# Tile 0 centred from sums, key weights first, and a reordered tail of phase one in a transformer block's forward and backward kernel

## The chip, the core and the metric

The kernel runs on one core of one Trainium2 chip. The metric is the device time in microseconds (us) of one execution. The engines are TensorE (PE; its weight loads are PEld), VectorE (DVE), ScalarE (ACT), GpSimd (POOL) and SyncE (SP, which here only issues transfers).

## The reference

All inputs are bf16. The block has S = 2048 rows and D = 640 columns; H = 32 heads of 20; F = 1728.

```
layernorm(x) = (x - mean) / sqrt(var + 1e-5)            # per row
phi(t) = where(t > 0, t + 1, exp(t)) + 1e-6
q, k, v = split(layernorm(x) @ wqkv)                     # per head
kv = sum_s phi(k)^T v ;  z = sum_s phi(k)
h  = x + ((phi(q) @ kv) / (phi(q) . z + 1e-6)) @ wo
out = h + (silu(layernorm(h) @ w1) * (layernorm(h) @ w3)) @ w2
```

The kernel returns `out` and, for a given `grad_out`, the gradients of x, wqkv, wo, w1, w3 and w2: seven outputs.

## The kernel before, in words

Rows are worked on in 16 tiles of 128 (`ST`). The order of the work on each engine is the order in which the program is written: no scheduler reorders it, and the buffers and their waits are set by the builder.

**Start.** x tile 0 is loaded first, then `load_x` and `load_wq` calls load the other x tiles and halves of wqkv (320 columns each; halves 2 and 3 are the key weights). 34 matmuls on ones (`WARM`) run on PE meanwhile. Tile 0 gets its statistics on DVE (`ln1.part`: two `bn_stats`, one `bn_aggr`, then the variance plus epsilon, whose power -0.5 is taken by POOL, line 154). `center_first` subtracts the mean, 256 columns on DVE and 384 on ACT; the factor 1/sigma is applied later, as the scale of phi's exp and relu, and to x itself by `p1_scale` at t = 3. `RAW` is the number of tiles treated so. All others are normalised by `p1_norm` (subtract and multiply, in place).

**Phase one.** A loop over t multiplies tile t with the key weights (`p1_mm`), applies phi (exp and relu on ACT; the rest, lines 298 and 299, on DVE, held back in a list and done later by a step `R`) and stores `pk_all`. Tiles below 8 are transposed on PE (`p1_tr`) inside the product of the tile before; from 8 on by a transposing DMA on SP. `v_steps` writes out by hand which DVE work is done in which t: `S` statistics, `N` normalising, `C` scaling, `R` phi's rest; `A`, `B` and `L` normalise after phi, after `q_tile`, and last. `outs` and `trickle` give the bulk transfers for a t. `m_part` accumulates phi(k)^T x; the first chunks of the gradient product `ghh_chunk` (grad_out times w2 transposed) fill in.

**The end of phase one** is written out line by line: `q_tile` (phi(q) of a tile), `r_prod` and `r_row` (the denominators; on POOL and DVE), `m_part`, and `kvT_block` (five matmuls into a buffer of tag `big`, and a masked copy to `bd` on DVE, line 211). Then PSUM pool `p1p` (tags `tr` 2, `big` 2 double ones, `m` 2) is released, and pool `pap` (`mm` 4, `at` 2, `o2` 2) takes its place. Its first work is `q_late(10)`, with five transposes (`f2_mT`, line 717, tag `at`) between its halves.

**MLP.** Four chunks c of 512 rows times 14 chunks fc of 128 columns, n = 14 c + fc: `mlp` multiplies with w1 and w3, DVE multiplies the pairs (`mlp_pair`, line 829), and `mlp_ghh` makes the gradient chunk n + 2 (`AHEAD`) from n = 6 on. In between, `sides` puts the next chunk's attention output (`f2_at`, line 654), its normalising (`f2_hn`) and its transposed form (`f2_ht`), and `r_steps` the denominators of tiles 8 to 15 (`r_den`, lines 366 and 373, whose products from tile 8 on lie in PSUM buffers of tag `at`) and transfers.

The backward products follow and are not touched.

Of the kernel before, what the change touches and what calls it, by code (L numbers as in the profile page):

```python
# [55 lines left out]
def kernel(  # L56
# [128 lines left out]
    def load_x(a, b):  # L185
        dma(out=x_sb[:, a:b, :], in_=xS[:, a:b, :])

    load_x(1, 2)
    A.activation(sg[:], zero[:], AF.Exp)
    load_wq(2, 3)  # L190
    load_x(2, 3)
    load_wq(3, 4)
    load_x(3, 4)
# [45 lines left out]
    XT_DMA = 8  # L239
    WARM = 34  # L240
    RAW = 1

# [9 lines left out]
    def p1_tr(t, parts=((0, DT),)):  # L252
        xn = x_sb[:, t, :]
        for a, b in parts:
            tr = ps.tile([P, DT, P], BF16, name="tr", bufs=2)
            for c in range(a, b):
                T.transpose(tr[:, c, :], xn[:, c * P:(c + 1) * P], ident[:])

            A.copy(out=pqT[:, a:b, t * P:(t + 1) * P], in_=tr[:, a:b, :])  # L259
# [200 lines left out]
    load_g2T(0)  # L460
    load_x(8, 12)
    load_w2T(2 * P, 4 * P)
    load_wq(0, 2)
    load_x(12, ST)
    def warm_up(n, warm):
# [4 lines left out]
    def center(t, a=0, b=D):  # L470
        ln1.center(x_sb[:, t, a:b], x_sb[:, t, a:b], t)

    nmean = cp.tile([P, 1], F32, name="nmean")

    def center_first():
        V.tensor_scalar(out=nmean[:], in0=ln1.mv[:, 0, 0:1], scalar1=-1.0, scalar2=None, op0=ALU.mult)
        center(0, 0, 2 * P)
        A.activation(out=x_sb[:, 0, 2 * P:], in_=x_sb[:, 0, 2 * P:], func=AF.Identity, bias=nmean[:, 0:1])

# [4 lines left out]

    ln1.part(x_sb, 0, 0)
    ln1.part(x_sb, 0, 1, center_first)
    p1_tr(0, ((0, 2), (2, DT)))
    warm_up(8, p1_acc()[:, 0])
    stat(1)
    p1_norm(1)  # L490
    ln1.part(x_sb, 2, 0)
# [10 lines left out]
    def load_wo():  # L502
        dma(out=wo[:], in_=A_wo.rearrange("(c p) n -> p c n", p=P))

    trickle = {4: w13[0], 5: w13[1], 9: lambda: load_wq(4, 6), 12: w13[2], 14: w13[3]}

    R = None
    v_steps = {1: (R, ("N", 4)), 2: (("S", 5), R, ("N", 5)), 3: (("S", 6), R, ("N", 6), ("C", 0)),
               4: (("S", 7), R, ("N", 7), ("S", 8)), 5: (R, ("N", 8), ("S", 9)), 6: (R, ("N", 9), ("S", 10)),
               7: (("S", 11), R, R, ("A", 10), ("L", 11)), 8: (("S", 12), R, R, ("S", 13)),  # L510
               9: (("N", 13), R, ("S", 14), ("B", 12)), 10: (R, R, ("S", 15)), 11: (R, ("B", 14), ("L", 15))}
    V_OPS = {"S": stat, "N": p1_norm, "C": p1_scale}
# [8 lines left out]

    outs = {7: ((xn_out, 0, dma),), 8: ((group_out, 0),), 12: ((group_out, 1), (xn_out, 1, dma)), 13: ((group_out, 2),)}

# [3 lines left out]
    for t in range(ST):  # L527
        first = None
        if t < RAW:
            first = phi_tiles()  # L530
            kh = [ps.tile([P, 512], F32, name="k0", tag="m", bufs=2) for _ in range(2)]

            def act(i, j):
                A.activation(first[i][:, j * HD:(j + 1) * HD], kh[j][:, 0:HD], (AF.Exp, AF.Relu)[i],
                             scale=ln1.rs[:, t:t + 1])

            def between():
                act(0, 0)
                p1_tr(t + 1)
                act(1, 0)  # L540
            k = p1_mm(t, D, between, kh)
            act(0, 1)
            act(1, 1)
        else:
            k = p1_mm(t, D, (lambda: p1_tr(t + 1)) if t + 1 < XT_DMA else None)
# [80 lines left out]
    q_tile(8)  # L626
    kvT_block(1, big())
    r_row(4)
    r_prod(6)
    phi_rest()  # L630
    m_part(4, range(5, 11))
    q_tile(9)
    phi_rest()
# [111 lines left out]
    def f2_hn(t):  # L745
        hn[t] = (pf.tile([P, D], BF16, name="hn", tag="pql", bufs=4) if t == 2 else
                 pf.tile([P, D], BF16, name="hn", tag="h2", bufs=2) if t == 3 else
                 pf.tile([P, D], BF16, name="hn") if t % 2 else w2[:, FT, :])
        ln2.norm(hn[t][:], x_sb[:, t, :], t)
        if t < 2:  # L750
            f2_ht(t)
        for n in ((), (0, 1))[t] if t < 2 else (t,):
            dma(out=hn_v[:, n, :], in_=hn[n][:])
# [29 lines left out]
    def mlp(c, fc, between):  # L783

        k, i = divmod(fc, 2)
        n = c * FT + fc
        if n >= FILL - AHEAD:
            mlp_ghh(n + AHEAD)
        gp = mm5(w1, fc, hnT[c])
# [169 lines left out]
    def sides(c):  # L959
        side = ({}, {})  # L960
        for i in range(TPC):
            k0 = 3 * i - (i == TPC - 1) * (1 + (c == 1)) + (-2, 1, 0)[c]
            for k, pos, f in ((k0 + 2, 1, f2_at), (k0 + 3, 0, f2_hn), (k0 + 3, 1, f2_ht)):
                if c == 0 and f is f2_at:
                    if i == 0:
                        continue
                    f = f2_at0
                if k0 == -2 and f in (f2_at0, f2_hn, f2_ht):
                    k, pos = (k + 1, 0) if f is f2_at0 else (k + 1, pos)
# [11 lines left out]
    def r_end(t):  # L981
        r_scale(t)
        r_out(t)

    r_steps = [{0: ((load_x, 6, 8),), 1: ((r4_out, 0, 2),), 2: ((r_load, 8),), 3: ((load_w2T, 10 * P, F),), 4: ((r_load, 9), (r4_out, 2, 4)),
                5: ((r_store, 7, 8),),
# [6 lines left out]
    for c in range(SC):  # L993
# [4 lines left out]
        def run_side(pos, fc):  # L998
            if c + 1 < SC:
                for f, i in sorted(sides[c][pos].get(fc, ()), key=lambda x: (x[0] is f2_ht, x[1])):  # L1000
                    f((c + 1) * TPC + i)
# [597 lines left out]
```

## Time and profile before

| | |
|---|---|
| median of 3 runs | 822.12 us (821.39 to 822.13) |
| the profiled execution | 820.91 us |
| its span, first to last instruction | 819.1 us |
| PE busy | 814.1 us (99%) |
| DVE busy | 452.4 us (55%) |
| ACT busy | 323.6 us (40%) |
| POOL busy | 130.9 us (16%) |
| granted TensorE clock | 1.0 in the span's mean |

The profile is one execution taken by the hardware profiler. A line of its timeline gives the start in us, the duration, the engine and source line, the operation, what it writes and reads, and, in brackets, how long the engine stood idle before it and what ended that. Durations of consecutive instructions overlap, since an engine starts the next one before the last has written everything: starts, not durations, tell the pace. L12 is line 12 of the kernel before.

### The profile page before, as it was taken

The page shows a single profiled execution, that of the slowest core. Times are in us where ns is not written, and L with a number is a line of the kernel's source. Part 1 is how long each engine was busy: PE and PEld are TensorE (multiplying, and loading weights), DVE is VectorE, ACT ScalarE, POOL GpSimd, SP SyncE. Part 2 cuts the span into 40 slices and gives each one's busy share as a digit, 9 for nine tenths or more (in the row PEclk, how much of TensorE's full clock was granted, in tenths as well). Part 3 has the DMA queues.
Part 4 walks back from the last instruction along what each step waited for, and adds up shares of the span by engine and source line. Part 5 has one row for each costly group of instructions (what it writes and reads, how often), then busy time and mean ns, then how long its engine had stood idle before and what let it go on. Part 6 is the DMA issues. An engine that isn't in the chain of part 4 may idle for free.

```text
span 819.1 us, 13944 instructions
## 1 busy us (share of the span) xinstructions
PE 814.1 (99%) x5420; PEld 512.8 (63%) x5420; DVE 452.4 (55%) x973; ACT 323.6 (40%) x603; POOL 130.9 (16%) x193
## 2 busy tenths in 40 slices
PE   9999999999999999999999999999999999999998
PEld 6677544555555555777777777777777777544444
DVE  7859987998898566300057777772781544200000
ACT  7856688665565666011122212222212334211111
POOL 2233333333222212100001111110220000000000
PEclk9999999999999999999999999999999999999999
DMA  9899699796485556999977877259974997967751
GB/s 264 219 290 239 166 244 327 225 245 173 127 211 156 169 170 167 222 261 226 257 176 180 211 197 200 58 107 187 287 195 93 181 194 159 239 164 186 160 141 36
DMA packets 323873, 157.88 MB, mean 193 GB/s; under 512 B 242784, under 2 KB 317056, under 8 KB 323808
## 3 DMA queue, kind: packets, MB, share of 16 engines
q1 hardware_dynamic: 281040, 116.18, 61.6%
q0 software_dynamic: 7328, 24.48, 8.7%
q10 hardware_dynamic: 35440, 16.34, 7.7%
q8 instruction: 42, 0.69, 0.4%
q14 instruction: 23, 0.19, 0.1%
HBM read 47.09 MB, written 51.13 MB: 120 GB/s over the span
## 4 chain that ended last, share of the span: by engine, by line
PE 96%; DVE 2%; ACT 1%; issue 0%; DMA 0%; POOL 0%; ACTq 0%; DVEq 0%
PE mm L394 20%; PE job L1346 20%; PE ghn L1142 14%; PE gxn L1515 8%; PE gw L1097 7%; PE o L910 4%; PE o L856 3%; PE gwo L1230 3%; PE big L267 3%; PE gr L1199 3%; PE dkv L1452 3%; PE macc L429 2%; PE at L654 2%; PE mm L267 1%; PE dkv L1380 1%; DVE st L147 1%
## 5 line engine op out<-in xcount | busy, mean ns | idle before, releaser
L1346 PE MATMUL job<-gb,hnN 128*128 128x496 bf16 (+3 forms) x576 | 116.8, 366 | 0.0
L1142 PEld LDWEIGHTS <-ggb 128*128 128x128 bf16 x864 | 84.5, 98 | 32.8
L1346 PEld LDWEIGHTS <-hnN 128*128 128x128 bf16 x576 | 55.8, 98 | 61.0
L394 PE MATMUL mm<-pqT,w 128*128 128x512 bf16 x405 | 93.8, 379 | 0.1
L394 PEld LDWEIGHTS <-w 128*128 128x128 bf16 x540 | 52.5, 98 | 63.4 <-issue 1.4
L1350 ACT CAST obs<-job 128x496 bf16<-128x496 f32 (+4 forms) x56 | 28.5, 510 | 123.7 <-PE job L1346 120.9
L1142 PE MATMUL ghn<-w13a,ggb 128*128 128x320 bf16 x448 | 63.5, 299 | 0.0
L1157 DVE SCALAR_TENSOR_TENSOR wb<-gs,hnb 128x640 f32<-128x640 bf16 x16 | 13.2, 825 | 88.7 <-ACT gs L1154 88.7
L1142 PE MATMUL ghn<-w13b,ggb 128*128 128x320 bf16 x416 | 61.4, 299 | 0.0
L394 PE MATMUL mm<-g2T,w2T 128*128 128x512 bf16 x240 | 59.6, 379 | 0.0
L1097 PE MATMUL gw<-g,hb 128*128 128x320 bf16 x416 | 56.8, 299 | 0.0
L1207 POOL TENSOR_TENSOR sz<-Zb,g_h 128x640 f32<-128x640 bf16 x16 | 20.2, 1261 | 197.7 <-DVE g_h L1208 197.7
L1097 PEld LDWEIGHTS <-hb 128*128 128x128 bf16 x416 | 40.6, 98 | 16.0 <-issue 0.3
L419 ACT CAST ghh<-mm 128x512 bf16<-128x512 f32 x48 | 28.3, 589 | 47.7 <-PE mm L394 40.1
L793 ACT ACTIVATE sig<-mm 128x512 bf16<-128x512 f32 x56 | 33.9, 605 | 26.4 <-PE mm L394 21.1
L1154 ACT ACTIVATE gs<-ghn 128x640 bf16<-128x640 f32 x16 | 11.3, 704 | 78.8 <-PE ghn L1142 73.9
L394 PEld LDWEIGHTS <-w2T 128*128 128x128 bf16 x260 | 25.4, 98 | 23.4
L267 PEld LDWEIGHTS <-pqT 128*128 128x128 bf16 x320 | 30.7, 98 | 13.7 <-ACT pqT L259 1.5
L267 PE MATMUL big<-wqkv,pqT 128*128 128x320 bf16 x250 | 38.6, 299 | 0.6 <-ACT pqT L259 0.3
L1346 PEld LDWEIGHTS <-g 128*128 128x128 bf16 x320 | 31.0, 98 | 11.5
L829 DVE TENSOR_TENSOR gate<-gate,sig 128x1024 bf16<-128x1024 bf16 x28 | 19.3, 689 | 33.2 <-ACT gate L804 30.5
L910 PE MATMUL o<-w,hhT 128*128 128x320 bf16 x224 | 35.0, 299 | 0.0
(219 smaller groups left out, 1369.9 us busy)
## 6 DMA issues: line engine op xcount, KB each, us to landing
hh_d<-hhT SPq DMA_DIRECT2D x24, 256.0 KB, 2.7
gg_d<-gate POOLq DMA_DIRECT2D x24, 256.0 KB, 4.3
gg_d<-ghh POOLq DMA_DIRECT2D x24, 256.0 KB, 3.4
ggb<-gg_d SPq DMA_DIRECT2D x6, 896.0 KB, 5.4
ggb<-gg_d ACTq DMA_DIRECT2D x6, 832.0 KB, 5.7
ggb<-gg_d SPq DMA_DIRECT2D x2, 1728.0 KB, 12.7
x_sb<-in_A_x_dram SPq DMA_DIRECT2D x5, 640.0 KB, 5.9
pk_d<-pk_all SPq DMA_DIRECT2D x4, 640.0 KB, 6.6
```

What stands on the lines that cost most here:

```text
L267: T.matmul(acc, lhsT=pqT[:, c, t * P:(t + 1) * P], rhs=wqkv[:, c, n0:n0 + HD], start=(c == 0), stop=(c == DT - 1))
L394: T.matmul(acc[:], lhsT=w[:, c, fc * P:(fc + 1) * P], rhs=rhs[:, c, :], start=(c == 0), stop=(c == DT - 1))
L419: A.copy(out=ghh[n // 2][:, n % 2, :], in_=acc[:])
L793: A.activation(sig[:, i, :], gp[:], AF.Sigmoid)
L856: T.matmul(accs[i, j][:, 0:HD], lhsT=hhT[c][:, fc, i * P:(i + 1) * P], rhs=w2[:, fc, j * HD:(j + 1) * HD], start=(first and fc == 0), stop ...
L910: T.matmul(o2["ps"][:, 0:HD], lhsT=hhT[c][:, fc, i * P:(i + 1) * P], rhs=w2[:, fc, j * HD:(j + 1) * HD], start=(fc == 0), stop=(fc == FT - 1))
L1097: T.matmul(acc[:, j, 0:HD], lhsT=hb[b][:, t, i * P:(i + 1) * P], rhs=g2[:, t, j * HD:(j + 1) * HD], start=(t == 0), stop=(t == ST - 1))
L1142: T.matmul(acc[:, j, 0:HD], lhsT=ggb[t // 2][:, k, lo:lo + P], rhs=rhs[:, j * HD:(j + 1) * HD], start=(k == 0), stop=(k == NG - 1))
L1199: T.matmul(gr[t][:, j, 0:HD], lhsT=ghT[t][:, c, :], rhs=wT2[:, c, j * HD:(j + 1) * HD], start=(c == 0), stop=(c == DT - 1))
L1346: T.matmul(acc[:, 0:n], lhsT=lhs[:, t, m * P:(m + 1) * P], rhs=rhs(t), start=(t == 0), stop=(t == ST - 1))
L1350: A.copy(out=ob, in_=acc[:, 0:n])
L1515: T.matmul(acc[:, j, 0:HD], lhsT=g, rhs=wqT[:, k, j * HD:(j + 1) * HD], start=(k == 0), stop=(k == 14))
```

## The change

- Tile 0's mean is made of two half sums: ACT copies columns 320 to 639 with a running sum, DVE reduces columns 0 to 319; `nmean` is minus their sum over 640. The centred tile goes to a buffer `xc` and x tile 0 stays as it is; its statistics (`stat(0)`) follow.
- `RAW` is 2: tile 1 is only centred, and phi takes its scale. At t = 3, tile 0 is normalised in x and tile 1 is scaled.
- The two key weight halves are loaded ahead of x tiles 1 and 2. The warm-up matmuls are 30 and 4 instead of 34 and 8.
- The load of x tiles 8 to 15 is split after 10 instead of 12; a load of w3 moves from t = 5 to 7, a store of `pk_all` from t = 8 to 9; tile 14 is normalised before `q_tile(3)` instead of after.
- `kvT_block(1)` moves behind `r_row(4)`, `r_prod(6)`, `phi_rest` and six tiles of `m_part`.
- From tile 4 on `f2_ht` is called in `f2_hn`, not half a chunk later. From n = 14 on `mlp_ghh` works one chunk ahead, and n = 14 itself has none. A transposing load of w2 and the load `r_load(8)` change places.

```diff
@@ -185,11 +185,11 @@
     def load_x(a, b):
         dma(out=x_sb[:, a:b, :], in_=xS[:, a:b, :])
 
+    load_wq(2, 3)
     load_x(1, 2)
     A.activation(sg[:], zero[:], AF.Exp)
-    load_wq(2, 3)
+    load_wq(3, 4)
     load_x(2, 3)
-    load_wq(3, 4)
     load_x(3, 4)
     load_x(4, 8)
 
@@ -237,8 +237,8 @@
     Z = cp.tile([P, DT], F32, name="Z")
 
     XT_DMA = 8
-    WARM = 34
-    RAW = 1
+    WARM = 30
+    RAW = 2
 
     def on_act(t):
         return t > XT_DMA and t % 2 == 0
@@ -250,7 +250,7 @@
             dmaT(out=pqT[:, :, t * P:(t + 1) * P], in_=xn)
 
     def p1_tr(t, parts=((0, DT),)):
-        xn = x_sb[:, t, :]
+        xn = x_sb[:, t, :] if t else xc[:]
         for a, b in parts:
             tr = ps.tile([P, DT, P], BF16, name="tr", bufs=2)
             for c in range(a, b):
@@ -458,10 +458,10 @@
     zero_pads()
     load_w2T(0, 2 * P)
     load_g2T(0)
-    load_x(8, 12)
+    load_x(8, 10)
     load_w2T(2 * P, 4 * P)
     load_wq(0, 2)
-    load_x(12, ST)
+    load_x(10, ST)
     def warm_up(n, warm):
         for _ in range(n):
             T.matmul(warm[:, 0:P], lhsT=ones[:], rhs=ones[:], start=True, stop=True, skip_group_check=True)
@@ -470,24 +470,29 @@
     def center(t, a=0, b=D):
         ln1.center(x_sb[:, t, a:b], x_sb[:, t, a:b], t)
 
+    xc = p1.tile([P, D], BF16, name="rq", bufs=3)
+    sums = cp.tile([P, 2], F32, name="sums")
     nmean = cp.tile([P, 1], F32, name="nmean")
 
     def center_first():
-        V.tensor_scalar(out=nmean[:], in0=ln1.mv[:, 0, 0:1], scalar1=-1.0, scalar2=None, op0=ALU.mult)
-        center(0, 0, 2 * P)
-        A.activation(out=x_sb[:, 0, 2 * P:], in_=x_sb[:, 0, 2 * P:], func=AF.Identity, bias=nmean[:, 0:1])
+        x0 = x_sb[:, 0, :]
+        A.activation(out=xc[:, HD:], in_=x0[:, HD:], func=AF.Identity, accum_out=sums[:, 1:2])
+        V.reduce_sum(out=sums[:, 0:1], in_=x0[:, 0:HD], axis=AX.X)
+        V.tensor_scalar(out=nmean[:], in0=sums[:, 0:1], scalar1=sums[:, 1:2], scalar2=-1.0 / D, op0=ALU.add, op1=ALU.mult)
+        V.tensor_scalar(out=xc[:, 0:2 * P], in0=x0[:, 0:2 * P], scalar1=nmean[:, 0:1], scalar2=None, op0=ALU.add)
+        A.activation(out=xc[:, 2 * P:], in_=x0[:, 2 * P:], func=AF.Identity, bias=nmean[:, 0:1])
 
     def stat(t):
         ln1.run(x_sb, t, t + 1)
         if on_act(t):
             ln1.bias(t)
 
-    ln1.part(x_sb, 0, 0)
-    ln1.part(x_sb, 0, 1, center_first)
+    center_first()
+    stat(0)
     p1_tr(0, ((0, 2), (2, DT)))
-    warm_up(8, p1_acc()[:, 0])
-    stat(1)
-    p1_norm(1)
+    warm_up(4, p1_acc()[:, 0])
+    ln1.part(x_sb, 1, 0)
+    ln1.part(x_sb, 1, 1, lambda: center(1))
     ln1.part(x_sb, 2, 0)
     ln1.part(x_sb, 2, 1)
     ln1.part(x_sb, 3, 0)
@@ -502,13 +507,13 @@
     def load_wo():
         dma(out=wo[:], in_=A_wo.rearrange("(c p) n -> p c n", p=P))
 
-    trickle = {4: w13[0], 5: w13[1], 9: lambda: load_wq(4, 6), 12: w13[2], 14: w13[3]}
+    trickle = {4: w13[0], 7: w13[1], 9: lambda: load_wq(4, 6), 12: w13[2], 14: w13[3]}
 
     R = None
-    v_steps = {1: (R, ("N", 4)), 2: (("S", 5), R, ("N", 5)), 3: (("S", 6), R, ("N", 6), ("C", 0)),
+    v_steps = {1: (R, ("N", 4)), 2: (("S", 5), R, ("N", 5)), 3: (("S", 6), R, ("N", 6), ("N", 0), ("C", 1)),
                4: (("S", 7), R, ("N", 7), ("S", 8)), 5: (R, ("N", 8), ("S", 9)), 6: (R, ("N", 9), ("S", 10)),
                7: (("S", 11), R, R, ("A", 10), ("L", 11)), 8: (("S", 12), R, R, ("S", 13)),
-               9: (("N", 13), R, ("S", 14), ("B", 12)), 10: (R, R, ("S", 15)), 11: (R, ("B", 14), ("L", 15))}
+               9: (("N", 13), R, ("S", 14), ("B", 12)), 10: (R, R, ("S", 15)), 11: (R, ("A", 14), ("L", 15))}
     V_OPS = {"S": stat, "N": p1_norm, "C": p1_scale}
 
     def xn_out(g, q):
@@ -519,14 +524,14 @@
         sl = slice(g * TPC, (g + 1) * TPC)
         dma(out=pk_v[:, sl, :], in_=pk_all[:, sl, :])
 
-    outs = {7: ((xn_out, 0, dma),), 8: ((group_out, 0),), 12: ((group_out, 1), (xn_out, 1, dma)), 13: ((group_out, 2),)}
+    outs = {7: ((xn_out, 0, dma),), 9: ((group_out, 0),), 12: ((group_out, 1), (xn_out, 1, dma)), 13: ((group_out, 2),)}
 
     QT = (6, 7, 9, 11)
     M0 = {7: (0, 1, 2), 8: (3, 4, 5)}
     M0.update({t: (t - 3,) for t in range(9, ST)})
     for t in range(ST):
         first = None
-        if t < RAW:
+        if t == 0:
             first = phi_tiles()
             kh = [ps.tile([P, 512], F32, name="k0", tag="m", bufs=2) for _ in range(2)]
 
@@ -624,11 +629,11 @@
     r_prod(5)
     m_part(4, range(5))
     q_tile(8)
-    kvT_block(1, big())
     r_row(4)
     r_prod(6)
     phi_rest()
     m_part(4, range(5, 11))
+    kvT_block(1, big())
     q_tile(9)
     phi_rest()
     for j in range(2):
@@ -747,7 +752,7 @@
                  pf.tile([P, D], BF16, name="hn", tag="h2", bufs=2) if t == 3 else
                  pf.tile([P, D], BF16, name="hn") if t % 2 else w2[:, FT, :])
         ln2.norm(hn[t][:], x_sb[:, t, :], t)
-        if t < 2:
+        if t < 2 or t >= TPC:
             f2_ht(t)
         for n in ((), (0, 1))[t] if t < 2 else (t,):
             dma(out=hn_v[:, n, :], in_=hn[n][:])
@@ -784,8 +789,8 @@
 
         k, i = divmod(fc, 2)
         n = c * FT + fc
-        if n >= FILL - AHEAD:
-            mlp_ghh(n + AHEAD)
+        if FILL - AHEAD <= n < FT or n > FT:
+            mlp_ghh(n + (AHEAD if n < FT else 1))
         gp = mm5(w1, fc, hnT[c])
         if i == 0:
             pair[k] = [ew(name) for name in NAMES]
@@ -960,12 +965,12 @@
         side = ({}, {})
         for i in range(TPC):
             k0 = 3 * i - (i == TPC - 1) * (1 + (c == 1)) + (-2, 1, 0)[c]
-            for k, pos, f in ((k0 + 2, 1, f2_at), (k0 + 3, 0, f2_hn), (k0 + 3, 1, f2_ht)):
+            for k, pos, f in ((k0 + 2, 1, f2_at), (k0 + 3, 0, f2_hn)):
                 if c == 0 and f is f2_at:
                     if i == 0:
                         continue
                     f = f2_at0
-                if k0 == -2 and f in (f2_at0, f2_hn, f2_ht):
+                if k0 == -2 and f in (f2_at0, f2_hn):
                     k, pos = (k + 1, 0) if f is f2_at0 else (k + 1, pos)
                 if k >= 0:
                     side[pos].setdefault(k, []).append((f, i))
@@ -982,7 +987,7 @@
         r_scale(t)
         r_out(t)
 
-    r_steps = [{0: ((load_x, 6, 8),), 1: ((r4_out, 0, 2),), 2: ((r_load, 8),), 3: ((load_w2T, 10 * P, F),), 4: ((r_load, 9), (r4_out, 2, 4)),
+    r_steps = [{0: ((load_x, 6, 8),), 1: ((r4_out, 0, 2),), 2: ((load_w2T, 10 * P, F),), 3: ((r_load, 8),), 4: ((r_load, 9), (r4_out, 2, 4)),
                 5: ((r_store, 7, 8),),
                 10: ((xn_out, 2, dmaG),), 12: ((r_load, 10),)},
                {0: ((r_den, 8), (load_x, 8, 12)), 1: ((r_end, 8), (r_load, 11), (xn_out, 3, dmaG)), 2: ((r_den, 9),), 3: ((r_end, 9), (r_load, 12)),
@@ -997,7 +1002,7 @@
 
         def run_side(pos, fc):
             if c + 1 < SC:
-                for f, i in sorted(sides[c][pos].get(fc, ()), key=lambda x: (x[0] is f2_ht, x[1])):
+                for f, i in sorted(sides[c][pos].get(fc, ()), key=lambda x: x[1]):
                     f((c + 1) * TPC + i)
 
         for fc in range(FT):
```

## The prediction

> **What bounds the kernel now.** I read the page's busy shares first, then who TensorE (PE) waited for, then the timeline at the places the change touches.
>
> ```profile
> span 819.1 us, 13944 instructions
> PE 814.1 (99%) x5420; PEld 512.8 (63%) x5420; DVE 452.4 (55%) x973; ACT 323.6 (40%) x603; POOL 130.9 (16%) x193
> ...
> DVE  7859987998898566300057777772781544200000
> ```
>
> ```profile
> PE warm L467 <- DVE zero L124: 1.1, 1, 1.1
> PE big L267 <- ACT pqT L259: 0.3, 1, 0.3
> ```
>
> PE is never idle long, so its program order sets the end. A busy PE hides short waits, so I also took the start-to-start distances of consecutive matmuls against the pace of the long streams here (fifteen of 512 columns in 3.24 us, 0.216 each; ninety of 320 in 12.22, 0.136). By that, PE loses 4.1 us in the first 20 us and afterwards only in five places more than 0.1 us: 0.28 at 37.7, 0.25 at 96.0, 0.16 at 97.5, 0.28 at 102.0, 0.15 at 548.7. So the change can win at most the start plus about 1.1 us, and it loses whatever new pause it puts into PE's order. VectorE (DVE) is the engine to watch: its digits are 9 and 8 in many slices.
>
> The start:
>
> ```profile
> 3.19 0.89 DVE L147 BATCH_NORM_STATS2 st<-x_sb 128x6 f32<-128x320 bf16 x2 [1.93 <-DMA x_sb<-in_A_x_dram]
> ...
> 4.36 0.15 DVE L476 TENSOR_SCALAR nmean<-ln_mv 128x1 f32<-128x1 f32 x1
> 4.43 0.28 DVE L157 TENSOR_SCALAR x_sb<-x_sb,ln_mv 128x256 bf16<-128x256 bf16 x1
> 4.55 0.62 ACT L478 ACTIVATE x_sb<-x_sb,nmean 128x384 bf16<-128x384 bf16 x1 [2.25 <-DVE nmean L476]
> ...
> 4.76 0.96 PE L257 MATMUL tr<-ident,x_sb 128*128 128x128 bf16 x5
> ...
> 6.37 1.20 PE L267 MATMUL k<-wqkv,pqT 128*128 128x320 bf16 x5
> ```
>
> The reader sees the chain arrival, statistics, mean, centring, transposes, first product. The end of the first phase, in time order across engines:
>
> ```profile
> 68.61 0.47 PE L448 MATMUL bigx<-mT,wqkv 128*128 128x140 bf16 x5
> ...
> 72.56 0.29 DVE L211 TENSOR_TENSOR bd<-bigx,mask 128x140 bf16<-128x140 f32 x1
> ...
> 72.77 0.86 DVE L373 TENSOR_REDUCE rden<-pr 128x16 f32<-128x320 f32 x2
> ...
> 73.94 0.51 PE L717 MATMUL trm<-ident,hx 128*128 128x128 bf16 x5
> ...
> 75.46 0.31 DVE L298 TENSOR_SCALAR mq<-mq 128x640 bf16<-128x640 bf16 x1
> ...
> 76.29 0.32 DVE L298 TENSOR_SCALAR mq<-mq 128x640 bf16<-128x640 bf16 x1
> ```
>
> DVE runs almost four us behind PE here: the product of `kvT_block(1)` is done at 69.08, its masked copy (L211) starts at 72.56. And in the MLP's second chunk row:
>
> ```profile
> 143.00:184.80 41.80, 41.80 (x230) 22.31 (x229) 40.69 (x84) 26.41 (x50) 12.80 (x19) 1.00 0.87 236
> ```
>
> The columns are PE, PEld, DVE, ACT and POOL busy: DVE 40.69 of 41.80 us, as full as PE.
>
> **The change part by part.**
>
> *Tile 0's mean by sums.* Removed from the front of the chain: two statistics and an aggregate (3.19 to 4.33). In their place DVE reduces 320 elements (nearest row L373, 128x320: 0.48) beside ACT, which copies 320 with a running sum. ACT from SBUF took 0.62 for 384 and 0.92 for 640, so 0.54 for 320; the accumulator read behind L1154 takes 0.19 and starts 0.10 before its ACTIVATE ends. Sum: 3.19 + 0.54 + 0.09 = 3.83 against DVE's 3.67. `nmean` (0.15 + two hand-overs of 0.035) ends the wait: centring starts at 4.06 on DVE instead of 4.43, and on ACT 0.49 earlier. Transposes begin near 4.38 and the first product near 5.8 instead of 6.37. The shorter warm-ups (30 and 4) fill those two waits and cost nothing: 30 matmuls end by 4.3.
>
> *What becomes of that 0.5 us.* Tile 0's statistics now follow on DVE, and tile 1 is only centred, which takes it off POOL's power (L154, 0.55, for which DVE stood idle 0.67). DVE: centre 4.06, statistics 4.25 to 5.17, aggregate and variance to 5.47, statistics of tile 1, centring at 6.63, statistics of tile 2 at 6.99, against 7.02 before. So DVE is where it was, if x arrives. It may not: the weight half of 410 KB now goes ahead of tile 1, which landed at 3.58 before and the half at 5.81; in the new order tile 1 takes the half's place (5.4 to 5.8) and tile 2 the second half's place (6.9 to 7.35). DVE then shifts by 0 to +0.36; I take +0.15, between the two orders' landings. From 10.9 to 34.3 DVE has no pause but its own hand-overs, so this shift stays.
>
> *Tile 0 normalised late, tile 1 scaled late.* The step at t = 3 was one scaling (L263); it becomes a normalising (0.44, next start 0.36 later) and the scaling: +0.36 on the same full DVE. The cover is PE's reserve on DVE's transposes (0.54 at 21.5), which holds; it ends at the pause at 37.7, where PE waits for ACT's relu, which waited for DVE (ACT idle 0.97 before 36.73). There the DVE shift comes through whole: 0.36 + 0.15 = **+0.5 us**, ends 0.3 and 0.8. Tile 1's two ACT passes with a scale (0.79 against 0.70) add 0.18 to ACT early, which PE sees as 0.08 at most and within the same 0.5.
>
> *Transfers.* w3's first half (832 KB) goes from t = 5 to t = 7, the stores of `pk_all` from t = 8 to 9. That puts 832 KB instead of 640 KB in front of the transposed rows of tiles 12 and 13 on SP's queue; tile 12's landed 0.11 us before PE needed it at 40.1. 192 KB more at some 340 GB/s (the first loads ran at 326 to 349) is 0.55 us less 0.11 of reserve; the 0.5 from above delays rows and PE alike. Ends 0 and +0.45; I take **+0.15**. Tile 14's norm on ACT ahead of `q_tile(3)`: 0.92 us of ACT where PE's next need is over 1.2 us off: nothing. The x split, `load_w2T` before `r_load(8)`, and `f2_ht` beside `f2_hn`: these rows land earlier or chunks ahead of use: nothing, and at worst what stood behind them on SP moves by one issue (1.2 us) under a reserve of chunks.
>
> *`kvT_block(1)` behind `phi_rest` and six tiles of `m_part`.* PE's order loses nothing. But on DVE its masked copy moves behind `r_row(4)` (72.77 to 75.46) and the two operations of tile 8's phi (75.46 to 76.29). It starts 3.52 later, at 76.08, and ends at 76.37. Who waits: the copy frees a `big` pair, and the next PSUM pool's tiles come to lie on those of the old (2 `tr`, 2 double `big`, 2 `m` against 4 `mm`, 2 `at`, 2 `o2`). The trace's semaphores have the first transpose of `f2_mT` (L717, tag `at`) wait for DVE, and the only DVE reader of the old buffers is L211. Its reserve is 73.94 - 72.85 = 1.09. So 3.52 - 1.09 = **+2.4 us** of PE pause. If the pair were the other one, `q_late(10)`'s second half at 74.29 would wait instead: 2.1. Nothing later gives it back: DVE and ACT are again waiting for PE by 82 (DVE 0.58 before 81.85).
>
> By the rows, is PE as fast after such a pause? The 34 warm-up matmuls of 128 columns took 0.107 us each and the five of 320 at 6.37 took 1.20, at 7.69 0.84: the full pace came about 7.1 us, some 6 us after PE's first work. No pause after that exceeds 0.5 us, so no row shows a loss of pace. [...]
>
> *One gradient chunk less ahead.* From n = 14 the ghh chunk is made one ahead, not two: chunk 14 loses five 512-column matmuls (1.08 us) and PE arrives 1.08 earlier at all that follows, until the last chunks even it out. DVE is full until 184.8 and can follow by only 0.39 (its pause there). The tightest place is `f2_at` at 190.50, which takes a buffer that DVE's `r_red` (189.85, first half done 190.33) frees: reserve 0.16. So 1.08 - 0.39 - 0.16 = **+0.55 us**, ends 0 and 0.9. No other reserve under 1.08 lies between 143 and 330 us.
>
> **Sum.** 0.5 + 0.15 + 2.4 + 0.55 = +3.6 us. The profiled execution took 820.91 (span 819.1 + 1.8), so it would take 824.5. The three runs' median is 822.12, 1.2 above it; on that scale 825.7. With all low ends +2.4 (824.5), with all high ends +4.6 (826.7).
>
> **Rivals.**
> A, *not slower*: the masked copy gates nothing, because the pool hands `kvT_block(1)` a buffer that is covered late, or the wait is short. Place: L717 at 73.94; price: -2.4, leaving +1.2, 823.3, within 0.2%. It decides from a pause under 0.45 us. For it: the buffers are picked by the program's builder, which the trace doesn't show for the new order. Against: all eight places are reused within 2 us.
> B, *faster*: the 0.5 us of the earlier first product survives and no shift of DVE reaches PE, and A holds: -0.5, 821.6. Against it: DVE full from 10.9 to 34.3. Even with all later pauses gone it would be 820.5.
> C: after the 2.4 us pause PE works at the warm-up's pace for as long as at the start: up to half of 6 us, +3.0: 828.7. For it: the slow start; against: short pauses left the pace alone.
>
> **Numbers.** About 0.2% (1.64 us) is what a measurement of this kernel can tell from no change. Forecast 0.79, A 0.10, B 0.03, C 0.05, the rest slower for small reasons. Likeliest 825.7, its own range 824.4 to 826.8. To leave out no more than two in ten and take in A: 823.2 to 827.3. Slower 0.87, same 0.11, faster 0.02.
>
> **What would show it.** Right: PE idle over 2 us before L717, released by DVE's L211; that L211 starting right behind tile 8's L299; a pause of half a microsecond before `at` in the MLP's second chunk row; a first product near 5.8, and `q_tile(3)` yet later than 38.1. Wrong: no PE wait at L717, or its transposes starting at 73.9 or earlier.

## The result and the profile after

The changed kernel takes 828.32 us in the median of six runs (826.48 to 829.96); the kernel before, beside it, 821.77 (821.31 to 823.79). The ratio is 1.0076, with a 95% interval of 1.0060 to 1.0093: slower by 6.55 us, where the forecast was +3.6 and the range ended at 827.3. Five of the six runs have a mean granted clock of 0.997 or 0.998; the sixth, at 1.000, took 826.48. The profiled execution took 828.32 us (clock 0.998) with a span of 826.5, against 819.1 before.

The page after, its head and DVE's row of the 40 slices (20.7 us each):

```profile
span 826.5 us, 13891 instructions
...
PE 813.4 (98%) x5384; PEld 512.3 (62%) x5412; DVE 454.1 (55%) x975; ACT 324.8 (39%) x605; POOL 130.8 (16%) x193
...
DVE  7858898999888656400047777772681545200000
```

PE's busy time is that of before (814.1, within a few missing records). The span is 7.4 us longer, so nearly all of that is pauses or slow matmuls. Whom PE waited for after the change (engine, line, what it waited for: us in total, times, longest):

```profile
PE trm L722 <- DVE bd L211: 2.3, 1, 2.3
PE big L267 <- DMA pqT<-x_sb: 1.3, 1, 1.3
PE tr L257 <- DVE ln_ve L153: 1.2, 1, 1.2
PE warm L467 <- DVE zero L124: 1.1, 1, 1.1
PE trh L770 <- DVE hn L160: 0.6, 1, 0.6
PE tr L257 <- DVE x_sb L160: 0.5, 1, 0.5
PE mm L394 <- DMA pqT<-hn: 0.5, 1, 0.5
```

Before, only the line of the first warm-up exceeded 0.3 us. The new lines are the accounts of this document. (Lines behind 480 have moved by 5: L722 is the old L717, L770 the old L765.) Measured as in the prediction, by start-to-start distances of matmuls against the pace of long streams, the 7.4 us fall apart thus (rounded, they add up to 7.5):

| place in the changed kernel | us | forecast |
|---|---|---|
| start, as far as it reaches 40 us (`tr` waits; the first product is 1.1 us earlier and does not help) | 0.6 | 0.5 |
| rows of tile 14 at 45.1 us | 1.5 | 0.15 |
| `trm` at 75.9 us, waiting for L211 | 2.5 | 2.4 |
| matmuls at half pace, 79.0 to 82.5 us | 1.6 | 0 (rival C, +3.0) |
| `trh` and the matmul behind it, 101.8 to 105.2 us | 1.0 | 0 |
| MLP's second chunk row, at 196.4 us | 0.3 | 0.55 |

Each size is a difference between two single profiles. The experiments below show how much of them is the change's.

The forecast pause, in the timeline after:

```profile
75.33 0.84 PE L267 MATMUL mm<-wqkv,pqT 128*128 128x320 bf16 x5
...
76.43 0.97 DVE L380 TENSOR_TENSOR pql<-pql,rden 128x640 bf16<-128x640 bf16 x1
...
77.32 0.31 DVE L298 TENSOR_SCALAR mq<-mq 128x640 bf16<-128x640 bf16 x1
...
77.73 0.49 DVE L299 TENSOR_TENSOR hx<-mq,rq 128x640 bf16<-128x640 bf16 x1
78.14 0.30 DVE L211 TENSOR_TENSOR bd<-bigx,mask 128x140 bf16<-128x140 f32 x1
...
78.49 0.44 PE L722 MATMUL trm<-ident,hx 128*128 128x128 bf16 x5 [2.32 <-DVE bd L211]
```

The masked copy stands right behind tile 8's L299, as forecast, and PE's first transpose follows it by 0.05 us. What was not forecast comes next. Three stretches of the same trace (us of each, then PE, PEld, DVE, ACT and POOL busy with the number of instructions, then the granted clock, DMA share and GB/s):

```profile
75.63:79.04 3.41, 1.09 (x12) 0.74 (x10) 3.13 (x8) 0.56 (x3) 1.08 (x2) 1.00 1.09 213
79.04:82.46 3.42, 3.42 (x21) 2.50 (x19) 0.55 (x2) 2.72 (x7) 0.00 (x0) 0.50 0.76 275
82.46:85.87 3.41, 3.41 (x38) 2.73 (x36) 2.82 (x8) 2.15 (x7) 0.00 (x0) 1.00 0.02 5
```

PE was busy for 1.09 of the first 3.41 us; for the next 3.41 us the clock is 0.50, and the same matmul of 320 columns that starts every 0.136 us elsewhere starts every 0.267. By the clock alone that is half of 3.41, 1.7 us; against the same matmuls before, 1.6.

### The profile page after: what moved, and what is told of

It is laid out like the page before. It is cut to its first block, busy times and chain, and to the rows that moved or that the text cites. A ratio compares the mean times of both kernels' runs of the same rounds, so it can differ in the third digit from the quotient of the medians.

```text
span 826.5 us, 13891 instructions
## 1 busy us (share of the span) xinstructions
PE 813.4 (98%) x5384; PEld 512.3 (62%) x5412; DVE 454.1 (55%) x975; ACT 324.8 (39%) x605; POOL 130.8 (16%) x193
## 4 chain that ended last, share of the span: by engine, by line
PE 86%; DVE 10%; DMA 2%; issue 1%; ACT 1%; SPq 0%; POOL 0%; DVEq 0%; ACTq 0%
PE job L1351 19%; PE mm L394 16%; PE ghn L1147 14%; PE gxn L1520 8%; PE gw L1102 7%; PE o L861 3%; PE gwo L1235 3%; PE gr L1204 3%; PE dkv L1457 3%; PE o L915 2%; PE at L659 2%; DVE st L147 1%; DVE s L834 1%; PE macc L429 1%; PE mm L267 1%
## 5 line engine op out<-in xcount | busy, mean ns | idle before, releaser
L834 DVE TENSOR_TENSOR gate<-gate,sig 128x1024 bf16<-128x1024 bf16 x28 | 19.3, 689 | 34.6 <-ACT gate L809 31.9
```

Source lines behind the costliest of these rows:

```text
L834: V.tensor_tensor(out=out, in0=a, in1=b, op=alu)
```

## Experiments

All kernels of a group ran on one chip together with the kernel before; times are medians in us. Kernels named `b_` are the kernel before with one edit, those named `a_` are the changed kernel with one or several. The ratios are the record's own; they can differ from the quotient of the two medians, by up to 0.0007 (`a_t6_fill8`, `b_pool`).

| group | kernel | us | before beside it | ratio, 95% interval |
|---|---|---|---|---|
| 1 | `b_kvt` | 826.18 | 823.24 | 1.0031 (1.0018 to 1.0044) |
| 1 | `b_kvt_mid` | 824.75 | 823.24 | 1.0014 (1.0002 to 1.0026) |
| 1 | `a_kvt_back` | 825.13 | 823.24 | 1.0020 (1.0010 to 1.0031) |
| 1 | `a_warm` | 827.52 | 823.24 | 1.0050 (1.0033 to 1.0067) |
| 2 | `after_again` | 828.17 | 822.47 | 1.0070 (1.0057 to 1.0082) |
| 2 | `a_bulk_back` | 825.54 | 822.47 | 1.0041 (1.0027 to 1.0054) |
| 2 | `b_head` | 822.78 | 822.47 | 1.0007 (0.9998 to 1.0016) |
| 2 | `b_mlp` | 822.85 | 822.47 | 1.0002 (0.9993 to 1.0011) |
| 3 | `a_undo2` | 823.77 | 823.27 | 1.0011 (1.0003 to 1.0020) |
| 3 | `a_late` | 823.61 | 823.27 | 1.0007 (0.9998 to 1.0015) |
| 3 | `b_late` | 825.46 | 823.27 | 1.0030 (1.0017 to 1.0044) |
| 3 | `b_pool` | 824.70 | 823.27 | 1.0024 (1.0013 to 1.0035) |
| 4 | `b_t6` | 822.11 | 822.75 | 0.9992 (0.9982 to 1.0003) |
| 4 | `b_bulk` | 823.35 | 822.75 | 1.0012 (1.0001 to 1.0023) |
| 4 | `b_kvt_warm` | 824.77 | 822.75 | 1.0025 (1.0012 to 1.0038) |
| 4 | `a_t6` | 823.36 | 822.75 | 1.0006 (0.9997 to 1.0015) |
| 5 | `a_t6_fill8` | 823.09 | 822.56 | 1.0000 (0.9991 to 1.0010) |
| 5 | `b_few8` | 823.07 | 822.56 | 1.0005 (0.9995 to 1.0014) |

**The pause and the clock.** `b_kvt` moves the one call; `b_kvt_mid` moves it less far:

```diff
     q_tile(8)
-    kvT_block(1, big())
     r_row(4)
+    kvT_block(1, big())   # b_kvt_mid: here
     r_prod(6)
     phi_rest()
     m_part(4, range(5, 11))
+    kvT_block(1, big())   # b_kvt: here instead, as in the change
     q_tile(9)
```

> The kernel before with only kvT_block(1) moved behind r_row(4), r_prod(6), phi_rest and six tiles of m_part. Theory 1 (pause and clock): the masked copy L211 comes some 3.5 us later on DVE, PE pauses 2.4 us before the transposes of f2_mT, the granted clock falls to half for one stretch of 3.41 us behind the pause and takes another 1.7 us: +4.1 us, about 825.9 against 821.8, clock of the span about 0.998. Theory 2 (the pause alone; the slow matmuls of the changed kernel came from something else in it): +2.4 us, about 824.2, clock 1.000.

> The kernel before with kvT_block(1) moved less far, behind r_row(4) only. The masked copy starts 2.7 us later than before instead of 3.5; less the reserve of 1.09 us PE should pause about 1.6 us. If the clock falls only where most of a 3.41 us stretch is idle (1.6 is 47% of it): +1.6 us, about 823.4, clock 1.000. If any pause of more than a microsecond lets it fall: +3.3 us, about 825.1, clock 0.998.

In `b_kvt` PE loses 2.48 us before `trm`, as in the changed kernel. Its twelve runs fall into two halves: six at a clock of 0.998, median 827.07, and six at 1.000, median 825.16, 1.9 us apart, where half pace over 3.41 us gives 1.7. So both theories of the expectation were right in half of the runs each; theory 1 is the one that says why. In `b_kvt_mid` the pause is 1.65 us (forecast there: 1.6); of twelve runs one shows 0.998 and two 0.999. (0.999 need not mean a slow stretch in the work: in the profiled runs of `a_kvt_back` and `a_t6`, both at 0.999, the clock fell only for the last 0.9 us of the span, behind PE's last product.)

What decides in a given run? Wherever the clock's records show it change, it does so in steps of one grid of 3.41 us, whose place differs from run to run: in the changed kernel's profile at 3.95, 79.04, 82.46 and 826.56 us (22, 1 and 218 steps apart), in that of the kernel before at 7.09 and 819.46 (238 steps). Here is `b_kvt`, whose profiled run slowed down, by stretches of its grid:

```profile
74.91:78.32 3.41, 1.09 (x12) 0.77 (x11) 2.99 (x7) 0.56 (x2) 0.67 (x1) 1.00 1.12 230
78.32:81.73 3.41, 3.41 (x23) 2.72 (x21) 0.65 (x3) 2.30 (x7) 0.00 (x0) 0.50 0.86 246
```

And the changed kernel's second profile (`after_again`), in which the same pause of 2.48 us left the clock alone:

```profile
74.30:77.71 3.41, 2.70 (x20) 1.82 (x19) 3.27 (x7) 1.95 (x4) 2.08 (x3) 1.00 1.06 190
77.71:81.13 3.42, 1.80 (x18) 1.42 (x18) 2.18 (x6) 1.33 (x4) 0.00 (x0) 1.00 0.88 203
```

There the grid cut the pause in two, and PE was busy for 1.80 us of the emptier stretch (53%). The four profiled stretches that were followed by half pace in the midst of the work had PE busy for 1.09 and 1.09 (the changed kernel and `b_kvt`), 1.35 (`a_bulk_back`, at 5.3 us, where the start's two waits fell into one stretch) and 1.46 us (`b_pool`): 32 to 43%. The emptiest stretch that kept the clock is one of `a_kvt_back`, with 1.72 us (50%). `b_pool`'s and `a_kvt_back`'s:

```profile
30.53:33.94 3.41, 1.46 (x12) 0.83 (x10) 3.11 (x10) 1.07 (x2) 0.96 (x2) 1.00 1.10 151
33.94:37.35 3.41, 3.41 (x15) 1.85 (x14) 2.54 (x8) 1.34 (x3) 0.55 (x1) 0.50 1.03 351
...
45.50:48.91 3.41, 1.72 (x13) 1.19 (x13) 1.44 (x7) 0.66 (x3) 1.23 (x5) 1.00 1.12 285
48.91:52.33 3.42, 3.42 (x27) 2.45 (x26) 1.49 (x5) 2.54 (x4) 0.39 (x2) 1.00 1.06 412
```

The ends of the profiles, where PE runs out of work, agree. In the eighteen whose records show the clock fall there, it falls behind a stretch with 0 to 40% of work, and not behind the four stretches with 52 to 57% that stand one step earlier. So in these traces the bound lies between 43 and 50% of a stretch; the one with `b_kvt_mid`'s pause of 1.65 us had 56% in the profiled run and stays on the safe side of it. A stretch in which PE was idle for 57% (`b_pool`) was enough here; in the prediction's sum the pause of 2.4 us has no such cost.

`a_warm` and `b_kvt_warm` keep the pause but fill it with work that nobody reads:

```diff
             p1_half(acc[:, 0:HD], t, j * HD)
             if j == 0 and between is not None:
+                if t == 10:
+                    for _ in range(36):
+                        T.matmul(acc[:, HD:HD + P], lhsT=ident[:], rhs=ident[:], start=True, stop=True, skip_group_check=True)
                 between()
```

> The changed kernel with 36 matmuls of 128 columns, whose results nobody reads, put on PE right before the transposes of f2_mT, in unused columns of the PSUM tile of q_late(10)'s first half: 1.96 us of work at full pace inside the 2.4 us pause. The pause's end, set by DVE, stays. Theory 1: the clock stays at 1.000 and 1.7 us come back, about 826.6. Theory 2: no change, 828.3.

> The kernel before with only kvT_block(1) moved, and 36 matmuls whose results nobody reads in the pause. Theory 1: the pause's end stays where DVE sets it, +1.9 us as in the runs of b_kvt with the full clock, and the clock is 1.000 in all runs instead of six of twelve: ratio about 1.002 against 1.003. Rival (the clock has another cause): as many runs below 1.000 as b_kvt.

In `a_warm`, 36 matmuls take the place of the pause, and `trm` still waits for L211:

```profile
75.64 2.17 PE L696 MATMUL mm<-ident 128*128 128x128 bf16 x36
78.11 0.44 PE L725 MATMUL trm<-ident,hx 128*128 128x128 bf16 x5 [0.30 <-DVE bd L211]
```

All thirteen runs of the two kernels have a clock of 1.000, where `b_kvt` has six low clocks in twelve and the changed kernel eight in eleven. They lie within 1.0 us (`a_warm`) and 2.9 us (`b_kvt_warm`) of each other. `b_kvt_warm` has a median of 824.77, 2.0 us above before, and no second group. So the slow clock hangs on PE's idleness, and the later copy alone costs 2.0 us: theory 1 is shown. As a repair the filling wins little, since the wait for the copy stays: 1.0025 against `b_kvt`'s 1.0031. (`a_warm`'s 1.0050 against the changed kernel's 1.0076 and 1.0070 is not the clock's doing alone: the pause at 102 us, treated below, is gone there too.)

**Which part costs what.** The parts one at a time, and the change without its two costliest:

> The changed kernel once more, beside the kernels of this group. In the four kernels run so far the transfers of the first phase cost more pauses (30.6 us, 45 us, 104 to 107 us) than in the two profiles from before, so the change's cost is wanted from this group: ratio 1.006 to 1.009 if the larger part is the pause at f2_mT with the slow clock behind it (the clock below 1.000 in about half of the runs, as with kvT_block(1) alone, 1.8 us apart).

> The changed kernel with kvT_block(1) back in its old place. Theory 1: both the pause and the slow stretch go, -4.1 us, about 824.2 against 828.3, clock 1.000; the 1 us lost between 96 and 107 us stays if it has another cause and goes too (823.2) if it follows from the pause. Theory 2: -2.4 us, about 825.9.

> The changed kernel with the w3 half back at t = 5 and the first pk_all store back at t = 8. Theory 3 (tile 14's transposed rows lie behind these transfers on SP's queue): the pause of 1.2 to 1.9 us before big at 45 us, which all three profiles with the moved transfers show, goes; -1.5 us against the changed kernel if nothing takes its place. Rival: in the order of before a pause of 1.2 to 1.7 us at 30.6 us comes back (both profiles of kernels with the old transfers in the last group show it), and the time stays within 0.5 us of the changed kernel.

> The kernel before with only the start changed: tile 0's mean by sums, key weight halves first, tile 1 only centred, shorter warm-ups, tile 0 normalised and tile 1 scaled at t = 3. The first product should start near 5.0 us instead of 6.4; then a pause of 1.2 us for tile 1's transposes, since tile 1 lands later. By the prediction's step, +0.5 us, about 0.6 by the traces: 1.0007. Rival: the start gains its 1.4 us less 1.2, no change within 0.2 us.

> The kernel before with only the changes of the MLP: f2_ht called in f2_hn from tile 4 on, one gradient chunk ahead from n = 14, load_w2T before r_load(8). By the prediction's step +0.55 us at f2_at near 190 us; by the trace of the changed kernel 0.3 us: ratio 1.0004 to 1.0007. The 1 us lost between 96 and 107 us lies before all of this and should not depend on it; if the profile shows it here too, the change has nothing to do with it.

> The changed kernel with both kvT_block(1) and the two moved transfers back in their old places: what is left is the start, the split of the x load, tile 14's earlier normalising and the MLP part. If the parts add up, as 1.0007 for the start and 1.0002 for the MLP part alone say, the ratio is 1.001, about 0.8 us above before, and the clock 1.000. Rival: the parts meet (tile 14's early normalising or the x split cost too): 1.002 or more.

The edits are the hunks of the change: `b_head` the start with `RAW`, `WARM`, the order of the key weights and t = 3; `b_mlp` everything behind `f2_hn`; `a_kvt_back`, `a_bulk_back` and `a_undo2` the reverse of the one call, of the two entries in `trickle` and `outs`, and of both. The single ratios are 1.0031 (`kvT_block`), 1.0012 (transfers, `b_bulk` below), 1.0007 (start) and 1.0002 (MLP): together 1.0052, 4.3 us, of the 1.0070 that the whole change shows in group 2. With both undone the rest is 1.0011, and start plus MLP give 1.0009: these add up, and the x split and tile 14's earlier normalising show no cost beyond these intervals. `a_kvt_back` gives back 0.50% against `after_again` in the next group, 4.1 us, which is theory 1's figure. What does not add up are the transfers: +1.0 us alone (1.0012 of 822.75), 1.4 us between the medians of `a_kvt_back` and `a_undo2` (825.13 and 823.77, beside befores of 823.24 and 823.27), and 2.6 us between `after_again` and `a_bulk_back`. The intervals are some ±1 us each, so the 1.5 us that the sum lacks may lie there or in scatter; this stays open.

**Where the transfers bite.** Row t is here the transposing transfer of tile t. All five profiles with the moved transfers show row 14 late, and PE loses 1.0 to 1.9 us to it. In the changed kernel:

```profile
36.42 2.53 SPq L250 DMA_TRANSPOSE pqT<-x_sb  x2
38.99 0.59 SPq L525 DMA_DIRECT2D pk_d<-pk_all  x1
39.62 0.51 SPq L183 DMA_DIRECT2D wqkv<-in_A_wqkv_dram  x1
41.51 2.70 SPq L250 DMA_TRANSPOSE pqT<-x_sb  x2
...
46.67 1.12 PE L267 MATMUL big<-wqkv,pqT 128*128 128x320 bf16 x7 [1.31 <-DMA pqT<-x_sb]
```

The first pair are rows 13 and 12, the last pair rows 14 and 15. Between them stand the moved store (640 KB) and the 800 KB of `wqkv`, and by the trace's semaphores row 14 lands at 46.62; before, with the store ahead of rows 12 and 13, it landed at 44.36 and PE came for its weights at 44.47. The other side of the move is row 9: it stood behind the w3 half at t = 5, landed at 30.5 in the profile before (no pause) but at about 31.9 in `b_mlp` and `b_kvt`, with pauses of 1.2 to 1.3 us at 30.6. (All six profiles of the kernel before with other edits and this load at t = 5 on SP's queue lose 0.8 to 1.7 us there.) So the move takes row 9's occasional pause and gives row 14 a steady one. Four placements test this (in `b_late` and `a_late` the load that stood at t = 12 goes on to 13):

```diff
-    trickle = {4: w13[0], 5: w13[1], 9: lambda: load_wq(4, 6), 12: w13[2], 14: w13[3]}
+    b_bulk: 7: w13[1], and in outs 9: ((group_out, 0),) for 8:
+    b_t6:   6: w13[1]                (a_t6: this, in the changed kernel, with kvT_block(1) and the store back)
+    b_late: 12: w13[1], 13: w13[2]   (a_late: likewise)
+    b_pool: 5: w13[1], issued by dmaG instead of dma
```

> The kernel before with only the two transfers moved as in the change (w3 half to t = 7, first pk_all store to t = 9). Theory 3: row 9's pause goes (0.5 to 1.2 us gained on the mean of the runs) and row 14's comes (1.2 to 1.9 us at 45 us, with 0.4 us at row 12): +0.3 to +1.4 us, ratio about 1.001. The prediction's step for this part was +0.15. Rival: the loss of 2.6 us that undoing it gave back in the changed kernel shows here too: 1.003.

> The kernel before with only the w3 half moved from t = 5 to t = 6, which is behind row 9's transposing transfer and ahead of rows 10 to 15. Theory 3: row 9 lands by 29 us, its pause at 30.6 us (0 to 1.7 us in the old order) goes, rows 10 and 11 land 0.5 to 1 us later than before but inside their reserve, rows 12 to 14 as before, and nothing moves to 69 us: 0.5 to 1.2 us faster, ratio 0.9985 to 0.9995. Rival: row 10 takes over the pause: no change.

> The changed kernel with kvT_block(1) and the first pk_all store in their old places and the w3 half at t = 6. The start costs 0.3 to 0.6 us and the MLP part 0.2; row 9 waits for nothing in either order here, as PE comes to it later: about 1.001, no faster than before.

> The kernel before with only the w3 half moved from t = 5 to t = 12, behind the last transposed row. Theory 3: the pause of 1.2 to 1.7 us at 30.6 us that the kernels of before's order show in this case's later profiles goes, none comes at 45 us: 1.0 to 1.3 us faster than before, ratio 0.9985. Rival: the pause moves to 69 us (rows of mT behind the later loads): no change.

> The changed kernel with kvT_block(1) and the first pk_all store in their old places, and the w3 half neither at t = 5 nor at 7 but at t = 12, behind the last transposed row. Theory 3 (whatever bulk stands on SP's queue ahead of the transposed rows delays them): neither the pause of 1.2 to 1.5 us at 30.6 us (row 9, old order) nor the ones at 40.8 and 45.7 us (rows 12 and 14, new order) is left; the time is that of the kernel with both undone less about 1.2 us, near that of before or 0.5 us under it. Rival: the transfers that come later by this 0.8 MB delay the transposed loads of mT at 60 us, and the pause moves to 69 us.

> The kernel before with the same w3 half left at t = 5, but issued on GpSimd's queue instead of SP's. If order on SP's queue is what delays row 9: the pause at 30.6 us goes, 1.0 to 1.3 us faster. If the transfer engines are simply shared, the row is served beside the load and lands later than alone: half of the pause or all of it stays, 0 to 0.6 us faster.

`b_bulk`: no pause at row 9, 0.99 us at row 14 (44.7 us), +1.0 us in all: theory 3 (bulk ahead of the rows delays them), inside its bounds. `b_t6`: row 9 lands at 28.4 us, no row waits before 60 us. It is 0.6 us under before in the median, but its interval just includes 1. `b_late` fell to its rival, and clearly:

```profile
PE bigx L448 <- DMA mT<-hx: 2.3, 1, 2.3
```

With the 0.8 MB that come later a transposing transfer of `mT` is issued at 63.0 us and lands at 71.1 (before: 59.9 and 68.1), and PE loses 2.49 us at 68.6, worth 1.0030. This pause is another in place and cause, and it too has the clock: five of ten runs at 0.997 or 0.998 (median 826.2), five at 1.000 (823.9). `a_late` shows the same shift with 1.0 us, and its rows 9, 12 and 14 free; so theory 3 held for them and the rival for the rest. `b_pool` is worse than either expectation: its pause at row 9 is 2.1 us. Leaving SP's queue did not free the row. It landed 2.05 us after the load (30.71 and 32.76), as it did behind the load on SP's queue in `b_kvt` (29.88 and 31.89) and `b_kvt_mid` (30.21 and 32.26; in the profile before it was 0.8 us); the load itself was issued 0.5 to 0.6 us later and landed 0.5 to 0.8 us later than there. So, as far as one profile tells, the row waits for the bulk that is under way, on whichever queue, and not for its place on SP's queue alone. No version was shown to be faster than before; `b_t6` is the lowest, and it is 0.8% under the changed kernel's ratio. `a_t6` keeps the change's start and MLP part beside it: 1.0006, so nothing shows that they are worth keeping.

**The pause at 102 us.** It was expected to be foreign to the change. But every profile with the changed start and nothing filled in shows it (0.6 to 1.4 us before `trh`), `b_head`'s too, and of the others only `b_few8`, below (the rest 0.25 us at most). `trh` waits for DVE's `hn`, and tile 2's `hn` for its buffer (tag `pql`), which the store `r_d<-pql` (`r_store`, on POOL's queue) must first have read. In the changed kernel:

```profile
98.38 0.62 POOL L737 DMA_DIRECT2D r_d<-pql  x1
...
102.15 1.04 DVE L160 TENSOR_SCALAR hn<-x_sb,ln_mv,ln_rs 128x640 bf16<-128x640 bf16 x2 [0.63 <-POOL ln_rs L154]
```

The view names POOL's `ln_rs`, which had long ended (101.76); the store landed at 102.07. So it took 3.7 us, before the change 2.2. In all nine profiles with the pause this `hn` starts 0.08 us after the store's landing. The queues' view for 99 to 100 us shows what else is under way then:

```profile
q8 instruction: 1, 0.02, 8.6%
```

Queue 8, of kind instruction, carries 42 packets of 16 KB in the whole run, and the rows of PE and PEld are 10.8 thousand. From one packet to the next the changed kernel's trace has 253 of these rows in the mean (182 to 308), and 0 to 55 of DVE; so the packets are read here as fetches of PE's instructions, a block each. In the changed kernel a block is fetched at 99.4, 1.1 us after the store's issue; in the kernel before at 91.7, 0.5 us ahead of it. These two are the sixth block of their run, and ahead of it lie 1423 and 1419 rows of PE and PEld: nearly as many. The changed start has eight warm-up matmuls less, each with its weight load; if a fetch goes by the number of PE's instructions, every later one comes sixteen of them later in the work. Two kernels test it:

```diff
 b_few8:
-    WARM = 34
+    WARM = 30
-    warm_up(8, p1_acc()[:, 0])
+    warm_up(4, p1_acc()[:, 0])
 a_t6_fill8:
                 act(0, 0)
+                for _ in range(8):
+                    T.matmul(kh[1][:, HD:HD + P], lhsT=ones[:], rhs=ones[:], start=True, stop=True, skip_group_check=True)
                 p1_tr(t + 1)
```

> The kernel before with 30 and 4 warm-up matmuls instead of 34 and 8, and nothing else. Theory 4: the fetch near 93 us falls behind r_store's issue, the store takes 3.4 us or more, and PE pauses 0.6 to 1.2 us before trh or the matmul behind it: ratio 1.0007 to 1.0015. Rival: no pause there, 1.000 within 0.0004, since PE waits at both places of the start anyway.

> The kernel a_t6 with eight matmuls of 128 columns, whose results nobody reads, put on PE where it waits 1.2 us for tile 1 near 6 us. Theory 4 (the fetch of PE's instructions delays the store): the fetch near 95 us comes ahead of r_store's issue again, the store lands in about 2.2 us instead of 3.4 to 4.3, the pause before trh goes, 0.9 to 1.2 us faster than a_t6 (823.36 against 822.75 of before): ratio about 0.9995. Rival (something else of the changed start delays the store, its buffers for instance): the pause stays, 1.0006.

Eight warm-ups less in the kernel before, and nothing else, bring the pause. `b_few8`'s store, its `hn`, and whom its PE waited for longest:

```profile
93.25 0.62 POOL L732 DMA_DIRECT2D r_d<-pql  x1
...
97.73 0.80 DVE L160 TENSOR_SCALAR hn<-x_sb,ln_mv,ln_rs 128x640 bf16<-128x640 bf16 x2 [1.33 <-issue]
```

```profile
PE trh L765 <- DVE hn L160: 1.3, 1, 1.3
```

The store landed 4.4 us after its issue, with the fetch 2.2 us behind the issue. Eight more in the changed start take the pause away: in `a_t6_fill8` the fetch falls together with the issue, the store takes 2.4 us, and no wait for `hn` is among PE's long ones. Over all twenty profiles:

| fetch of PE's block, from the store's issue | store lands after | profiles |
|---|---|---|
| 5.4 to 4.0 us ahead | 2.2 us | `a_warm`, `b_kvt_warm` |
| 0.6 to 0.0 us ahead | 2.1 to 2.5 us | before, `a_t6_fill8`, seven `b_` kernels |
| 1.1 to 2.2 us behind | 3.4 to 4.4 us | after, seven more with its start, `b_few8` |

How the fetch holds up the store can be read from the trace's packets. The store's data are 32 packets of 5 KB. In the eleven profiles of the first two rows all 32 start between 1.2 and 1.8 us after the issue. In the nine of the last row thirty of them do; the next starts only 2.3 to 3.1 us after the issue, in each of the nine within 0.02 us of the fetch's end, and the last one after it. So two packets wait until the fetch is over, and the landing waits for them. In two of the nine (`a_late` and `b_few8`) the fetch itself begins 0.6 us after the thirty have started; what held the two packets until then stays open.

So the cause of the pause is shown, down to the number of PE instructions. In time it is worth less than the pause and is not clear of noise: `b_few8` and `a_t6_fill8` both have medians 0.5 us above before, with ratios of 1.0005 and 1.0000 whose intervals include 1, so the expected 0.9 to 1.2 us from `a_t6` to `a_t6_fill8` were not shown. In `a_t6_fill8` a pause of 1.1 us at 102.9 takes the place of the one that went, as the kernels with before's start have at 102 to 107 us too (0.3 to 1.3 us); the view names ACT's `up` (L807), which came late itself, and why it did was not settled.

## Why the prediction was wrong, step by step

- *Tile 0's mean by sums, what becomes of it, and tile 0 normalised late*: the forecast was +0.5, and 0.6 is what the profile shows at 40 us and what `b_head` measures (1.0007, interval -0.2 to +1.3 us). The path is another, so the agreement is partly luck. The first product comes at 5.3 instead of 6.4, earlier than the 5.8 forecast; PE then waits 1.2 us for tile 1, which now lands behind a weight half, and 0.5 us for tile 2, and by 13 us the loss is there. The pause at 37.7, through which the forecast led a shift of DVE to PE, does not grow: it is gone in the changed kernel. That the shorter warm-ups "cost nothing" was wrong in a way that no row near them shows: they moved an instruction fetch 90 us later onto a store, which gives a pause in the profiles, though nothing clear of noise in time.
- *Transfers*: the step that failed first. It weighed the moves on rows 12 and 13 alone and gave 0.15. The store at t = 9 stands ahead of rows 14 and 15 too, and row 14's reserve of 0.11 us was to be had from the trace. The part costs 1.0 us by itself and up to 2.6 within the change.
- *`kvT_block(1)`*: mechanism, releaser, place and size of the pause as forecast (2.4; 2.48 lost; 2.0 us in time where the clock holds). Rival A fell.
- *"Is PE as fast after such a pause?"*: the step that failed second. Rival C, at 0.05, came true in 14 of 23 runs (eight of eleven of the changed kernel, six of twelve of `b_kvt`), at 1.7 us and not 3.0: the slow stretch is one step of the clock's grid, and the chance is that of where the pause falls in it. By an estimate from the bound above (50 to 57% of a step idle) and the 2.32 us that PE is idle in the profile, this is so at 54 to 69% of the places in a step of 3.41 us. The sum put the term at nothing, which no run had shown for a pause this long (in the profile before none behind the start exceeds 0.5 us); it should have held about 1.0 us. The run of the changed kernel that kept the clock, 826.48, lies inside the forecast's range; in the second group the two that kept it took 827.59 and 828.17, beside a before of 822.47.
- *One gradient chunk less ahead*: 0.55 was forecast at `f2_at`; the wait there is 0.3 us in every profile with the part, and `b_mlp` measures +0.2 us with an interval from -0.6 to +0.9. Right place, size too high.

## What to carry to other kernels

A pause of PE of 2.48 us cost itself here, and in 14 of 23 runs another 1.7 us; by the profiles this is so where it leaves a step of the clock's grid of 3.41 us less than half full (43% and below in these traces). A pause of 1.65 us cost only itself in nearly all runs (one of twelve had a clock of 0.998). When a transfer is moved on a queue, check the reserve of every row that it newly stands ahead of, not of the nearest ones alone, and of the rows at the place it moves to: of five placements of one load (t = 5, 6, 7 and 12, and GpSimd's queue), four paid somewhere, at three different rows, and another queue did not help (a pause of 2.1 us in `b_pool`). Where PE waits for an engine that had long finished (here `ln_rs` at 101.76, with the store landing at 102.07), look for the transfer that holds the buffer, and at what the queues carried beside it.

## What the runs showed of the hardware that was not expected

- With one and the same start the full clock came between 4.4 us (`b_kvt_warm`) and 7.1 us (before), less than one step of the grid apart.
- The granted clock fell at the start too (`a_bulk_back`: 8.7 to 12.1 us), after two waits of 1.1 and 1.4 us within one step of the grid. So here two short waits counted like one long one.
- A fetch of 16 KB of PE's own instructions 1.1 to 2.2 us behind a small store goes with a landing 1.2 to 2.2 us later, in nine profiles of nine: two of the store's 32 packets start only when the fetch ends. Eight matmuls more or less at the start of the kernel moved the fetch across the store's issue, 90 us later.
